# Linear attention in front of an MLP on one core: sub-chunks of 64 tokens in place of 128, with the state advanced twice per chunk

## The chip, the cores and the metric

The kernel runs on one core of a Trainium2 chip. The metric is the device time of one execution in microseconds (us), and the time of a kernel is the median of its runs. The times of this case are of single runs that agree to a few parts in a thousand.

## The reference

Four batches, eight heads, 768 tokens, head dimension 64, all in fp32. Attention is linear and decays by a factor `lam` per head and token. The reference itself goes in blocks of 64 tokens and carries a 64 x 64 state from block to block; its output, with the heads side by side, is the input of an MLP.

```python
for b in range(nb):                      # 12 blocks of 64 tokens
    qb, kb, vb = (q[:, :, sl], k[:, :, sl], v[:, :, sl])
    intra = einsum('bhic,bhjc->bhij', qb, kb) * Dmask[None]      # lam**(i-j) for i >= j, else 0
    intra = einsum('bhij,bhjd->bhid', intra, vb)
    inter = einsum('bhid,bhde->bhie', qb * lam_pow[None], kv_state)
    out[:, :, sl] = intra + inter
    kb_dec = kb * rev_pow[None]
    kv_state = lam_block * kv_state + einsum('bhsd,bhse->bhde', kb_dec, vb)
...
x = out.transpose(0, 2, 1, 3).reshape(3072, 512)
h = x @ w_in                             # 512 -> 2048
out = (h - tanh(h)) @ w_out              # 2048 -> 512
```

## The kernel before

**Stages.** The 768 tokens are cut into six chunks of `BLK` = 128 tokens, and the kernel has six stages g = 0 to 5, one for each chunk of all four batches (512 tokens). In each stage attention makes x for the chunk, and the MLP follows. The MLP's matrix products are done by Strassen and Winograd's scheme of seven products on halves of the operands (`up` for w_in, `down` for w_out), some of them with a second such level inside (`inner_steps` for w_in, `down_twice` for w_out). The sums that the scheme needs are VectorE's (DVE's) work. The products with 128x128 tiles of weights are most of TensorE's (PE's) time. The factors of w_out are kept in DRAM and read again in each stage by GpSimd's (POOL's) queue, `send`, L676 to L696.

**Order.** No planner sets the order. It is the order of the program, written out by hand from L909 to L1086: functions with `yield` (`up_plain`, `down`, `down_twice`, `inner_steps`) are stepped by `next`, `steps` and `every`, and the attention functions stand between the steps. `tied` and `keep_in_program_order` hold an instruction at its place in its engine's queue. In stages from `GB` = 2 on, attention for the next chunk comes in two stretches for two batches each, `att_out(g + 1, (0, 1))` at L1037, after the fourth of `down(g, 2)`'s steps, and `att_out(g + 1, (2, 3))` at L1058, after the seven steps of `down_twice(g, 6)`. In stage 1 the same work for a pair of batches comes in three visits, between `up_plain`'s units (L949 to L972), in stage 0 at the start (L909 to L937).

**One pair of batches.** A matmul of attention is 64 wide in its contraction or its output, and so uses a quarter or a half of the 128x128 array; pairs of heads j = 0, 1 lie on partitions 0 to 63 and 64 to 127. NP = 4 such pairs p. `qt`, `kt` are q and k transposed; in stages 0 and 1 the transposes are PE's (L362) with ACT's copies (L364), later DVE's (L357) from blocked loads. `qd` is `qt` times the powers of lam, `fwd` (L368). The stretch then has, in PE's order:
- scores (`att_scores`, L382 and L384): k's two halves of 64 tokens against q, the first against both halves of q (128 columns), the second against the second alone, into two `sp` banks of tag `att`; DVE multiplies each by `mask` (L388, 128x384) into `ss`;
- state products (`att_read`, L428): `state` against `qd`, 64x64 by 128 columns, into two `op` banks (`ya`, `z`); after them ACT decays the state in place, four ACTIVATEs (L432);
- kv products (`kv_products`, L403): decayed k against v, all 128 tokens deep, into one bank (`yb`); k was decayed by `att_decay` (L394) beforehand;
- inner products (L457, 128 deep, for the second half of the chunk, and L468, 64 deep, for the first), v against `ss`, into the same `op` banks; L468 waits by hand for the first decay (L475);
- DVE adds kv to the state (L477), and ACT copies the `op` banks to `xt` (L479), which the MLP reads; `att_sums` and `inner_tokens` make sums of `xt` for its seven-product schemes.

The last stage has no kv products, no decay of k and loads no k (`nat`, L192).

**PSUM.** There are eight banks: four share the tag `att`, and `ya`, `yb`, `z` and `w` are one each. `down_twice` takes `ya` and `z` or `yb` and `w` for its products n (L780), so that one is read out while the next is made.

**Start.** Weights come as 64-bit words and are rounded in the kernel (`round_block`, L310 to L325, three ACT and some DVE instructions for a block). `mask` is made by eight scans (L110), `fwd` by doubling (`powers`, L116), in stage 1.

Each `nc.tensor.matmul` in fp32 shows in the profile as two MATMUL and two LDWEIGHTS records: 2960 calls make 5856 recorded MATMULs (a few records are missing).

Of the kernel before, what the change touches and what calls it, by code (L numbers as in the profile page):

```python
# [18 lines left out]
BLK = 128  # L19
GB = 2  # L20
# [4 lines left out]
def kernel(  # L25
# [65 lines left out]
    wide = const.tile([128, 192], F32, name="ident")  # L91
    ident = wide[:, 0:128]
    lam_all = const.tile([128, H], F32)
    fwd = const.tile([128, NP, BLK], F32)
    nc.vector.memset(fwd[:, 0, :], 0.0)
# [3 lines left out]

    HALF = BLK // 2
    nc.vector.tensor_copy(wide[:, 128:192], wide[:, 0:64])
    mask = const.tile([128, 2, 6, HALF], F32)
    whole = xpool.tile([128, 3, 2, HB], F32, name="whole", tag="tt").rearrange("s a b c -> s (a b c)")[:, 0:2 * DM].rearrange(
        "s (j p i) -> s j p i", j=2, p=NP)
    for j in range(2):
        for p in range(NP):
            h = 2 * p + j
            nc.vector.tensor_tensor_scan(out=whole[:, j, p, :], data0=lam_all[:, h:h + 1].to_broadcast([128, BLK]),  # L110
                                         data1=ident if p < 2 else wide[:, HALF:HALF + BLK], initial=0.0, op0=AL.mult,
                                         op1=AL.add)
    nc.vector.tensor_copy(mask[:, :, 2:6, :], whole[:, :, :, HALF:BLK])
    nc.vector.tensor_tensor(mask[:, :, 0:2, :], whole[:, :, 0:2, 0:HALF], whole[:, :, 2:4, 0:HALF], op=AL.add)

    def powers():  # L116
        for j in range(2):
            tc.keep_in_program_order(nc.vector.tensor_copy(
                fwd[ts(j, 64), :, 0], lam_all.rearrange("s (p j) -> s j p", j=2)[ts(j, 64), j, :]))
        m = 1  # L120
        while m < BLK:
            tc.keep_in_program_order(nc.vector.tensor_tensor(
                fwd[:, :, m:2 * m], fwd[:, :, 0:m], fwd[:, :, m - 1:m].to_broadcast([128, NP, m]), op=AL.mult))
            m *= 2


    bwd = mask.rearrange("s j p i -> s p j i")[:, 2:6, :, HALF - 1:HALF].to_broadcast([128, NP, 2, D])
# [15 lines left out]
    def load_natural(g, b, names):  # L143
        for name, src, bufs in (("q", q, 2), ("k", k, 3), ("v", v, 4)):
            if name in names:
# [7 lines left out]
                else:  # L153
                    eng = nc.sync if g > 0 else nc.scalar if b == 0 else nc.gpsimd
                    whole_ = {(0, 1, "k"): nc.scalar, (0, 2, "k"): nc.gpsimd}.get((g, b, name), nc.sync)
                    parts = [(eng, x[ts(1 - t, HALF), 4:8], rows[ts(t, HALF), 4:8]) for t in range(2)]
                    parts.insert(2 * (whole_ is nc.gpsimd), (whole_, x[:, 0:4], rows[:, 0:4]))
# [21 lines left out]
    def load(n):  # L179
# [3 lines left out]
        while at["loaded"] < min(n, len(chunks)):  # L183
# [8 lines left out]
            nat = "kv" if g < NG - 1 else "v"  # L192
# [147 lines left out]
    for _ in range(8):  # L340
        nc.tensor.matmul(out=idle[:, 0:128], lhsT=fwd[:, 0, :], rhs=fwd[:, 0, :], start=True, stop=True)


    state = const.tile([128, B, NP, D], F32)


    tr, sc, kdec, xt = {}, {}, {}, {}

    def att_transpose(g, bs):
        for b in bs:  # L350
# [14 lines left out]
            qd = None  # L365
            if g > 0:
                qd = work.tile([128, NP, BLK], F32, name="qd", tag="qd")
                nc.vector.tensor_tensor(qd, qt, fwd, op=AL.mult)  # L368
            tr[g, b] = (qt, kt, qd)

    def att_scores(g, bs):
        for b in bs:
            qt, kt, _ = tr[g, b]

            sp = [bank("sp", "att", 4)[:, 0:6 * HALF].rearrange("s (x i) -> s x i", x=6) for _ in range(2)]
            for p in (0, 2, 1, 3):
                x, r = p % 2, p // 2
                for j in range(2):
                    kj, qj = kt[ts(j, 64), p, :], qt[ts(j, 64), p, :]

                    k0, k1 = (kj[:, ts(t if r == 0 or g >= GB else 1 - t, HALF)] for t in range(2))
                    tied(g != 1, nc.tensor.matmul(out=sp[j][ts(r, HALF), x:3 + p:2 + p - x, :], lhsT=k0,  # L382
                                                  rhs=qj.rearrange("d (t i) -> d t i", t=2), start=True, stop=True))
                    tied(g != 1, nc.tensor.matmul(out=sp[j][ts(1 - r, HALF), 2 + p, :], lhsT=k1,  # L384
                                                  rhs=qj[:, HALF:BLK], start=True, stop=True))
            ss = work.tile([128, 2, 6, HALF], F32, name="ss", tag="ss")
            for j in range(2):
                op = tied(g != 1, nc.vector.tensor_tensor(ss[:, j], sp[j], mask[:, j], op=AL.mult))  # L388
            sc[g, b] = ss
        return op  # L390
# [5 lines left out]
    def kv_products(g, bs):  # L396

        kv = bank("kv", *(("yb", 1) if g >= GB else ("att", 4))).rearrange("d (b p e) -> d b p e", b=2, p=NP)
        for n, b in enumerate(bs):
            kd, vn = raw[g, b]["k"], raw[g, b]["v"]  # L400
            for p in range(NP):
                for j in range(2):
                    tied(g == 0, nc.tensor.matmul(out=kv[ts(j, 64), n, p, :], lhsT=kd[:, 2 * p + j, :],  # L403
                                                  rhs=vn[:, 2 * p + j, :], start=n == 0 and p == 0, stop=True,
                                                  skip_group_check=True))
        return kv

    def att_state(g, bs):
        kv = kv_products(g, bs)
        tied(True, nc.scalar.activation(state[:, bs[0]:bs[0] + 2], kv, AF.Copy))  # L410

    reads = {}

    def out_dst(ops, n, p, j):
        return ops[p // 2][ts(j if p < 2 else 1 - j, 64), p % 2, n, :]

    def att_read(g, bs):
        ops = [bank("op", *x).rearrange("d (p b s) -> d p b s", p=2, b=2)
               for x in ((("ya", 1), ("z", 1)) if g >= GB else (("att", 4),) * 2)]
        decayed = None  # L420
        if g > 0:
            st = state[:, bs[0]:bs[0] + 2]
            for n, b in enumerate(bs):
                for p in (0, 1):
                    for j in range(2):
                        r = ts(j, 64)
                        for pp in (p, p + 2):
                            nc.tensor.matmul(out=out_dst(ops, n, pp, j), lhsT=state[r, b, pp, :],  # L428
                                             rhs=tr[g, b][2][r, pp, :], start=n == 0 and p == 0, stop=False,
                                             skip_group_check=True)  # L430
            for p in (3, 2, 1, 0):
                op = tied(g == 1, nc.scalar.activation(st[:, :, p, :], st[:, :, p, :], AF.Copy,  # L432
                                                       scale=fwd[:, p, BLK - 1:BLK]))
                decayed = decayed or op
        reads[g, bs] = ops, decayed

    def att_out(g, bs):
        half = bs[0] // 2
        xt[g, half] = xpool.tile([128, KI, HB], F32, name=f"xt{half}", tag=f"xt{half}")
        st = state[:, bs[0]:bs[0] + 2]  # L440
        if g >= GB:

            att_scores(g, bs)
        if (g, bs) not in reads:
            att_read(g, bs)
        ops, decayed = reads.pop((g, bs))

        def dst(n, p, j):
            return out_dst(ops, n, p, j)

        if g >= GB:
            kv = kv_products(g, bs) if g < NG - 1 else None
        for n, b in enumerate(bs):
            ss, vn = sc[g, b], raw[g, b]["v"]
            for p in range(NP):
                for j in range(2):
# [660 lines left out]
```

## Time and profile before

| | |
|---|---|
| median of 3 runs | 659.21 us (657.57 to 659.94) |
| the profiled execution | 658.74 us, of which its span in the trace is 657.0 |
| PE, matmuls | 644.1 us busy, 98% of the span |
| PE, weight loads (beside the matmuls) | 590.7 us, 90% |
| DVE | 468.9 us, 71% |
| ACT | 243.7 us, 37% |
| POOL | 209.0 us, 32% |
| granted TensorE clock | 0.995 mean |
| instruction transfers (queue q8) | 47, 0.77 MB |

How PE's busy time lies over the stages, in us of each stretch of the span:

| from to | length | PE busy |
|---|---|---|
| 0 to 30 (start, stage 0) | 30.0 | 24.5 |
| 30 to 115 | 85.0 | 84.4 |
| 115 to 213 | 98.0 | 97.9 |
| 213 to 328 | 115.0 | 112.7 |
| 328 to 434 | 106.0 | 105.3 |
| 434 to 540 | 106.0 | 106.0 |
| 540 to 657 | 117.0 | 113.4 |

Times in lines of the trace count from the span's start. A line of PE's timeline gives start, length, engine, source line, operation, tiles as output<-moving,weights, the shape of the part of the array and of the data, and a count; what stands in brackets is the idle time before it and what ended it. The length of one matmul contains the time in which it lies in the pipe (L468's mean is 226 ns, though one starts every 15 to 20 ns), so the cost of a group of matmuls is read from start to start. "issue" as a releaser means that the engine waited for nothing that the profile shows.

### The profile page before, as it was taken

What the parts mean: (1) busy time and instruction counts of PE and PEld (TensorE: products, weight loads), DVE (VectorE), ACT (ScalarE), POOL (GpSimd) and SP (SyncE); (2) the same over time, 40 slices, a digit from 0 to 9 for tenths busy, and PEclk for the clock granted to TensorE, in tenths of its full rate; (3) what the DMA queues carried; (4) which work ended last, traced back from release to release, by engine and by line L of the source; (5) the groups of instructions that cost most, each with busy time, mean ns of one, the idle gap of its engine ahead of it and who ended that gap; (6) DMA issues with size and microseconds to landing.
All of it is one profiled execution on the core that took longest, in us unless ns stands there. A gap on an engine that the chain in (4) does not pass through costs nothing. (4 is left out here: it accounts for less than half of the span.)

```text
span 657.0 us, 15041 instructions
## 1 busy us (share of the span) xinstructions
PE 644.1 (98%) x5856; PEld 590.7 (90%) x5856; DVE 468.9 (71%) x889; ACT 243.7 (37%) x485; POOL 209.0 (32%) x362
## 2 busy tenths in 40 slices
PE   8899999999999999999999999999999999999998
PEld 7788888888888899988999988999988899998897
DVE  4457979968878785578776668789468687466663
ACT  2776766523321222532223452213453213263210
POOL 6000126766223335202335302243401164400241
PEclk7999999999999999999999999999999999999999
DMA  9869987988768768957656957576967476721374
GB/s 201 198 168 200 254 245 229 380 245 253 146 143 212 212 182 257 211 95 187 198 173 213 243 125 168 141 242 200 238 123 159 113 268 209 225 71 33 89 247 162
DMA packets 156951, 125.80 MB, mean 191 GB/s; under 512 B 127744, under 2 KB 130048, under 8 KB 156880
## 3 DMA queue, kind: packets, MB, share of 16 engines
q0 software_dynamic: 27168, 87.91, 43.8%
q1 hardware_dynamic: 128096, 36.53, 26.8%
q8 instruction: 47, 0.77, 0.5%
q10 hardware_dynamic: 1616, 0.39, 0.4%
q14 instruction: 24, 0.20, 0.1%
HBM read 103.81 MB, written 20.97 MB: 190 GB/s over the span
## 5 line engine op out<-in xcount | busy, mean ns | idle before, releaser
L691 POOL DMA_DIRECT2D wb<-fine x148 | 79.7, 539 | 189.8 <-PE y L788 63.2
L792 ACT ACTIVATE q<-y 128x128 f32<-128x128 f32 x96 | 26.6, 277 | 144.4 <-PE y L788 143.4
L788 PE MATMUL y<-wb,g 128*128 128x128 f32 x456 | 60.3, 277 | 0.7 <-DVE q L802 0.7
L843 PE MATMUL h<-xt,w 128*128 128x256 f32 x256 | 58.0, 383 | 2.0 <-DVE w L325 2.0
L843 PEld LDWEIGHTS h<-xt,w 128*128 128x128 f32 x256 | 47.6, 190 | 9.9 <-DVE w L325 3.2
L788 PEld LDWEIGHTS y<-wb,g 128*128 128x128 f32 x456 | 55.3, 192 | 1.2 <-issue 0.6
L694 POOL DMA_DIRECT2D wb<-factors x44 | 23.8, 541 | 83.1 <-PE y L733 50.8
L556 ACT ACTIVATE th<-g 128x512 f32<-128x512 f32 x40 | 25.2, 630 | 66.6 <-DVE g L574 50.7
L548 PE MATMUL y<-xt,w 128*128 128x256 f32 x192 | 45.0, 379 | 0.0
L388 DVE TENSOR_TENSOR ss<-sp,mask 128x384 f32<-128x384 f32 x48 | 23.7, 550 | 26.4 <-PE sp L384 26.4
L557 DVE TENSOR_TENSOR g<-g,th 128x512 f32<-128x512 f32 x40 | 27.6, 691 | 20.7 <-ACT th L556 20.7
L548 PEld LDWEIGHTS y<-xt,w 128*128 128x128 f32 x192 | 36.4, 190 | 5.1 <-ACT g L565 0.2
L788 PE MATMUL zw<-wb,g 128*128 128x128 f32 x304 | 40.3, 275 | 0.0
L548 PE MATMUL y<-tt,ws 128*128 128x256 f32 x160 | 37.8, 379 | 0.0
L548 PE MATMUL y<-tt,w 128*128 128x256 f32 x160 | 37.8, 379 | 0.0
L548 PE MATMUL z<-xt,ws 128*128 128x256 f32 x160 | 37.8, 379 | 0.0
L733 PE MATMUL y<-wb,g 128*128 128x256 f32 x160 | 37.3, 379 | 0.0
L788 PEld LDWEIGHTS zw<-wb,g 128*128 128x128 f32 x304 | 37.0, 192 | 0.2 <-DVE g L794 0.2
L733 PE MATMUL w<-wb,g 128*128 128x256 f32 x160 | 35.3, 379 | 0.0
L548 PEld LDWEIGHTS z<-xt,ws 128*128 128x128 f32 x160 | 30.4, 190 | 4.1
L733 PEld LDWEIGHTS y<-wb,g 128*128 128x128 f32 x160 | 30.4, 190 | 4.1
L733 PEld LDWEIGHTS w<-wb,g 128*128 128x128 f32 x160 | 30.4, 190 | 4.1
(206 smaller groups left out, 1469.4 us busy)
## 6 DMA issues: line engine op xcount, KB each, us to landing
wb<-fine POOLq DMA_DIRECT2D x148, 256.0 KB, 3.9
wb<-factors POOLq DMA_DIRECT2D x44, 256.0 KB, 4.7
wb<-fine_in POOLq DMA_DIRECT2D x36, 256.0 KB, 4.0
raw<-in_moe_w_out_dram SPq DMA_DIRECT2D x12, 512.0 KB, 6.4
rest<-fine POOLq DMA_DIRECT2D x20, 256.0 KB, 4.6
raw<-in_moe_w_in_dram SPq DMA_DIRECT2D x16, 256.0 KB, 6.4
fine<-f POOLq DMA_DIRECT2D x16, 256.0 KB, 4.7
q_blk<-in_q_dram SPq DMA_DIRECT2D x128, 32.0 KB, 3.3
```

The costliest lines, as they stand in the source:

```text
L388: op = tied(g != 1, nc.vector.tensor_tensor(ss[:, j], sp[j], mask[:, j], op=AL.mult))
L548: nc.tensor.matmul(out=t[:, m, :], lhsT=wt[:, kt, ts(m, 128)], rhs=x[:, kt, :], start=first and m == 0 and kt == 0, stop=kt == 1, skip_gro ...
L556: nc.scalar.activation(th, src, AF.Tanh)
L557: nc.vector.tensor_tensor(dst(c), src, th, op=AL.subtract)
L691: nc.gpsimd.dma_start(out=t.rearrange("p m c -> p (m c)"), in_=fine[TWICE.index(n_), SUB.index(x_)].rearrange("p u c -> p (u c)"))
L694: nc.gpsimd.dma_start(out=t, in_=factors[XAT[FACT[n_][1]]][:, 2 * x_:2 * x_ + 2, :])
L733: nc.tensor.matmul(out=t[:, m, :], lhsT=a[:, u, kt, ts(m, 128)], rhs=wb[:, kt, :], start=first and u == 0 and m == 0 and kt == 0, stop=u = ...
L788: tied(x == STEPS[-1], nc.tensor.matmul(out=dst, lhsT=a[:, u, :], rhs=wb[:, ts(u, 128)], start=x in (1, 2) and u == 0, stop=u == NU - 1, s ...
L792: nc.scalar.activation(keep, dst, AF.Copy)
L843: tied(u == 0, nc.tensor.matmul(out=hm[c][:, m, :], lhsT=w1[u][:, i, a, ts(m, 128)], rhs=xt[0, t][:, i, :], start=m == 0 and i == 0, stop= ...
```

## The change

Attention goes in sub-chunks of `HALF` = 64 tokens, like the reference; the stages stay at 128.
- `mask` and `fwd` are made for 64 tokens; scores are only those within a half, 16 products of 64x64x64 for each batch, and `ss` is 256 wide in place of 384. `row(j, t)` puts half t of head j on one half of the partitions, and k and v are loaded with the halves of the odd heads swapped. `fwd` is made at the start.
- `kv_products` makes the kv of each half of the chunk, in two banks, all as quarter products.
- `att_half` does the first half of a chunk: state products, four decays by ACT, scores (from stage 2 on), kv, inner products, and DVE's addition of the first kv to the state (a copy by ACT in stage 0). `att_out` then does inner and state products of the second half with the new state, and ACT's copies to `xt`. `att_state` comes later: four more decays, and the second kv is added.
- From stage 2 on the two halves of the output have two banks each: `ya` and `z` for the first, two `att` banks for the second. `down_twice`'s products 4 and 7 use `att` banks, so that kv can have `yb` and `w`.
- The last stage does kv for its first half, and so loads and decays k.
- `att_state` and part of `inner_tokens` are placed between the MLP's steps; the decay of k for the pairs of stage 1 and the first pair of stage 2 moves ahead.

```diff
-    fwd = const.tile([128, NP, BLK], F32)
+    fwd = const.tile([128, NP, HALF], F32)
+    state = const.tile([128, B, NP, D], F32)
...
-            nat = "kv" if g < NG - 1 else "v"
+            nat = "kv"
...
+    def row(j, t):
+        return ts(j if t else 1 - j, HALF)
...
-            for p in (0, 2, 1, 3):
-                x, r = p % 2, p // 2
-                for j in range(2):
-                    kj, qj = kt[ts(j, 64), p, :], qt[ts(j, 64), p, :]
-                    k0, k1 = (kj[:, ts(t if r == 0 or g >= GB else 1 - t, HALF)] for t in range(2))
-                    tied(g != 1, nc.tensor.matmul(out=sp[j][ts(r, HALF), x:3 + p:2 + p - x, :], lhsT=k0,
-                                                  rhs=qj.rearrange("d (t i) -> d t i", t=2), start=True, stop=True))
-                    tied(g != 1, nc.tensor.matmul(out=sp[j][ts(1 - r, HALF), 2 + p, :], lhsT=k1,
-                                                  rhs=qj[:, HALF:BLK], start=True, stop=True))
+            for p in range(NP):
+                for t in range(2):
+                    for j in range(2):
+                        kj, qj = kt[ts(j, 64), p, :], qt[ts(j, 64), p, :]
+                        tied(g != 1, nc.tensor.matmul(
+                            out=sp[j][row(j, t), p, :], lhsT=kj[:, ts(t, HALF) if g >= GB else row(j, t)],
+                            rhs=qj[:, ts(t, HALF)], start=True, stop=True))
...
+        tags = (("z", 1), ("w", 1)) if (g, bs) == (0, (0, 1)) else (("yb", 1), ("w", 1)) if g >= GB else (("att", 4),) * 2
+        kv = [bank("kv", *x).rearrange("d (b p e) -> d b p e", b=2, p=NP) for x in tags[:2 if g < NG - 1 else 1]]
...
+                for t in range(len(kv)):
+                    for j in range(2):
+                        tied(g != 1, nc.tensor.matmul(
+                            out=kv[t][ts(j, 64), n, p, :], lhsT=kd[row(j, t), 2 * p + j, :],
+                            rhs=vn[row(j, t), 2 * p + j, :], start=n == 0 and p == 0, stop=True, skip_group_check=True))
...
+    def out_banks(g, t=0):
+        def both(tags):
+            return [bank("op", *x) for x in tags]
+        if g >= GB:
+            two = both((("att", 4),) * 2 if t else (("ya", 1), ("z", 1)))
+            return None, [[x[:, 0:4 * HALF].rearrange("d (p b s) -> d p b s", p=2, b=2) for x in two]]
+        pair_ = both((("att", 4),) * 2)
+        views = [x.rearrange("d (p b s) -> d p b s", p=2, b=2) for x in pair_]
+        return views, [[x[:, :, :, ts(t, HALF)] for x in views] for t in range(2)]
+    def in_quarters(g, bs, make):
+        for n, b in enumerate(bs):
+            for p in (0, 1):
                 for j in range(2):
+                    for pp in (p, p + 2):
+                        op = tied(g != 1, make(n, b, pp, j, n == 0 and p == 0))
+        return op
+    def state_products(g, bs, ops, t):
+        return in_quarters(g, bs, lambda n, b, p, j, first: nc.tensor.matmul(
+            out=out_dst(ops, t, n, p, j), lhsT=state[ts(j, 64), b, p, :], rhs=tr[g, b][2][ts(j, 64), p, ts(t, HALF)],
+            start=t == 0 and first, stop=False, skip_group_check=True))
+    def inner_products(g, bs, ops, t, after=None):
...
+                out=out_dst(ops, t, n, p, j), lhsT=raw[g, b]["v"][row(j, t), 2 * p + j, :], rhs=sc[g, b][row(j, t), j, p, :],
...
+    def att_half(g, bs):
+        st = state[:, bs[0]:bs[0] + 2]
+        banks_, ops = out_banks(g)
         decayed = None
         if g > 0:
+            state_products(g, bs, ops, 0)
+            decayed = decay_state(g, bs)
+        if g >= GB:
+            att_scores(g, bs)
+        kv = kv_products(g, bs)
+        op = inner_products(g, bs, ops, 0, decayed)
+        if g == 0:
+            made = tied(True, nc.scalar.activation(st, kv[0], AF.Copy))
+        else:
+            made = tied(g >= GB, nc.vector.tensor_tensor(st, st, kv[0], op=AL.add))
...
     def att_out(g, bs):
...
+        if g >= GB:
+            att_half(g, bs)
         xt[g, half] = xpool.tile([128, KI, HB], F32, name=f"xt{half}", tag=f"xt{half}")
+        banks_, ops, kv = half_way[g, bs]
+        if g >= GB:
+            ops += out_banks(g, 1)[1]
+            inner_products(g, bs, ops, 1)
+            state_products(g, bs, ops, 1)
+        else:
+            state_products(g, bs, ops, 1)
+            inner_products(g, bs, ops, 1)
...
+    def att_state(g, bs):
+        if g == NG - 1:
+            return
...
+            decay_state(g, bs)
+        tied(g != 1, nc.vector.tensor_tensor(st, st, half_way[g, bs][2][1], op=AL.add))
...
     def down_twice(g, n):
...
-        y, zw = (("ya", "z") if n in (4, 6) else ("yb", "w")) if g == NG - 1 else ("ya", "z") if n in (5, 3) else ("yb", "w")
-        y, zw = bank("y2", y, 1)[:, 0:128], bank("zw", zw, 1)
+        if g == NG - 1:
+            y, zw = ("ya", "z") if n in (4, 6) else ("yb", "w")
+        else:
+            y, zw = {4: ("att", "att"), 7: ("att", "att"), 6: ("yb", "w")}.get(n, ("ya", "z"))
+        y, zw = bank("y2", y, 4 if y == "att" else 1)[:, 0:128], bank("zw", zw, 4 if zw == "att" else 1)
...
+        if not last and g < GI:
+            att_decays(g + 1, (0, 1))
         p2 = down(g, 2)
         steps(p2, NU)
         send(stream.index((g, 4, SUB[0])))
-        if not last and g < GI:
-            att_decays(g + 1, (0, 1))
+        next(p2)
         if not last:
             att_out(g + 1, (0, 1))
         every(p2)
         sums_twice(g, 5)
         p4 = down_twice(g, 4)
+        steps(p4, 3)
+        if not last:
+            att_state(g + 1, (0, 1))
...
+        if not last:
+            inner_tokens(g + 1, False)
         p6, p7 = down_twice(g, 6), down_twice(g, 7)
-        steps(p6, len(STEPS))
+        steps(p6, len(STEPS) + 1)
         if not last:
             att_out(g + 1, (2, 3))
         every(p6)
         steps(p7, 2)
         if not last:
+            att_state(g + 1, (2, 3))
             att_sums(g + 1, None)
```

## The prediction

> **What bounds the kernel now.** I read the page first, parts 1 and 2, for the engine that sets the end.
>
> ```profile
> span 657.0 us, 15041 instructions
> ...
> PE 644.1 (98%) x5856; PEld 590.7 (90%) x5856; DVE 468.9 (71%) x889; ACT 243.7 (37%) x485; POOL 209.0 (32%) x362
> ...
> PEclk7999999999999999999999999999999999999999
> ...
> q8 instruction: 47, 0.77, 0.5%
> ```
>
> TensorE (PE) is busy 98% of the span at full clock, so a change pays what it takes from PE or leaves PE waiting. The last line is used below: 47 transfers of 16 KB carry instructions, and 2 x 5856 records of PE over 47 is 249 per transfer, so they are in the main PE's own.
>
> The chain of waits runs along PE through every attention stretch (L382, L428, L403, L457, L468 one after the other). So I took PE's timeline for one such stretch, stage 4, second pair of batches; columns are start, length, engine, line, tiles, shapes, count.
>
> ```profile
> 441.95 0.32 PE L382 MATMUL sp<-qt,kt 64*64 64x128 f32 x1
> ...
> 443.33 1.05 PE L428 MATMUL op<-qd,state 64*64 64x128 f32 x32
> 444.32 1.15 PE L403 MATMUL kv<-v_nat,k_nat 128*64 128x64 f32 x32
> 445.30 1.10 PE L457 MATMUL op<-ss,v_nat 128*64 128x64 f32 x32
> 446.34 0.69 PE L468 MATMUL op<-ss,v_nat 64*64 64x64 f32 x32
> 446.96 0.60 PE L788 MATMUL y<-wb,g 128*128 128x128 f32 x3
> ```
>
> From start to start: scores 1.38 us, state 0.99, kv 0.98, tall inner products 1.04, short ones 0.62; 5.01 us for 192 records. Then the same view one stage earlier and in the last stage, where a stretch is longer:
>
> ```profile
> 342.99 0.34 PE L468 MATMUL op<-ss,v_nat 64*64 64x64 f32 x7
> 343.99 0.62 PE L468 MATMUL op<-ss,v_nat 64*64 64x64 f32 x25 [0.66 <-issue]
> ```
>
> ```profile
> 547.05 0.56 PE L468 MATMUL op<-ss,v_nat 64*64 64x64 f32 x21
> 548.00 0.45 PE L468 MATMUL op<-ss,v_nat 64*64 64x64 f32 x11 [0.38 <-issue]
> ```
>
> In the middle of one line's matmuls PE stood 0.66 and 0.38 us, released by "issue": no semaphore, no data. The transfer view around these moments has one instruction transfer each, 341.14 to 342.66 and 545.81 to 546.75. PE went on 1.33 and 1.25 us after their ends. A third pause of 0.74 us (241.29) also ends 1.26 us after such a transfer (239.07 to 240.03), though the profile names a DVE op there. I read these as PE having run out of instructions.
>
> **Part A, PE's work.** After the change all four products are 64x64x64 on quarters of the array. A pair of batches has 64 matmuls of each kind in two records: 4 x 64 = 256 records. Price: inside L468 the records' starts come in fours 6 to 8 ns apart, with a new four every 58 to 59 ns (446.70, 446.76, 446.81), so 14.6 ns a record. Entering the form costs some 0.05 us and leaving it 0.09 (L468's last start to L788's first is 0.148). So 256 x 14.6 = 3.73, + 0.14 = 3.87 us. The other bound is L468's whole group, 0.62/32 = 19.4 ns, 4.97 us; I take 14.6, since the kinds now follow each other in one form.
> - Stages 2 to 4, six stretches: 5.01 - 3.87 = 1.14 each, **-6.8**.
> - Last stage, two: now 4.23 (520.10 to 524.33, no kv). After: 192 x 14.6 = 2.80, and 32 kv records that use two quarters only, 58 ns per two as in L403, 0.93; with 0.14 3.87. **-0.7**.
> - Stage 1, two pairs, each in three visits: now 1.50 + 1.03 + 2.64 = 5.17; after 3.73 + 3 x 0.14 = 4.15. **-2.0**.
>
> Sum **-9.5**.
>
> **Part B, instructions.** A matmul call is two records and two weight loads, four instructions; 2960 calls now, 3344 after. A transfer holds some 256 instructions, 128 records. At the products of the MLP these last 128 x 0.112 = 14 us (L788: eight records in 0.89). In a stretch now they last 128 x 5.01/192 = 3.3 us; after, 128 x 14.6 ns = **1.87**. How fast can they come? After each of the three pauses, PE has just begun a block and the next transfer begins 1.59, 1.47 and 1.31 us later (345.58, 549.47, 242.60), takes 1.19, 1.33 and 1.20, and by the pauses the instructions can run 1.25 to 1.33 after its end: 4.1, 4.1 and 3.8 us from block to block. So a block that lies wholly in a stretch should cost 4.0 - 3.3 = 0.7 now (0.66, 0.38, 0.74 seen) and 4.0 - 1.87 = **2.1** after. A stretch now is 384 instructions, one and a half blocks, so some stretches hold no whole block; a stretch after is 512, two blocks, so each holds at least one. The block that sticks out brings its own cover, since beyond the stretch 64 instructions take 3.5 us. Stepping blocks of 256 through the program's order with these paces gives 14 to 24 us over the eight stretches by where the boundaries fall, about 17 in the middle. What is lost now goes out of this: 0.66 + 0.38 + 0.74, and 0.26 by which L468 at 213.48 (0.95) is longer than its usual 0.69: 2.0. **+15**, between +12 and +22. Stage 1 has at most 320 fast instructions in a row, and slow products around them: 0 to 1, taken as 0.
>
> **Part C, waits that the order adds.** The second half's state products wait for a DVE add (new L471) of the state, behind four ACT decays.
> - Stages 2 to 5: the decays (1.26 to 1.28 for four, L432) run beside scores; the mask products, four of 0.33 now that they are 256 wide (L801 has that size), end about when kv does; the add needs 0.6; PE meanwhile has 0.93 of inner products. 0 to 0.2 a stretch; behind the add are only DVE's MLP sums, due later. In the first stretch of stage 2, kv's second bank waits for the sum L759, and DVE is busy to 210.1: 0.3.
> - Stage 1, first pair: ACT now rounds to 74.0, decays 1.26, rounds again; DVE's first op on the w_out block stands ahead of the add in its queue, which so ends near 78.0. PE, with 3.46 us of products between, asks at 77.5: 0.5. Second pair: ACT reaches the decays at 95.09, behind the rounding L320 to L322; PE asks at 94.8: 0.6. DVE is held to 97.6 by L325 and L862, the add ends at 98.3, PE asks at 97.65: 0.7.
>
> Sum 2.2; a stretch that waits for instructions hides a part. **+1.5**, between 0 and 4.
>
> **Part D, at nothing.** Start: PE waits there for others (1.26 at 21.70 and 0.40 at 27.76, both for rounded weights behind ACT). The new state copy and products on ACT's way to the first xt (0.6 + 0.5) stand against 0.7 saved on products; one more block of instructions comes into these 20 us (64 calls). **+0.5**, from -1 to +2. DVE: 48 mask products shorter by 0.14; ten adds of 0.6, four decays in the last stage, four qd halves and two state products more: +4 in 188 us idle. ACT: eight more sets of decays and split copies, +13 in 413 idle. SP issues 12 more k loads in the last stage; k of 64 to 128 KB lands in 3.7 to 3.9, and its first reader is two units of products later. Products 4 and 7 go to the att banks, which DVE's mask products have freed by then; if not, up to the 0.74 seen at 241.29 each. POOL's weight loads follow PE's reads and shift with them. The token sums that move ahead, and the stage-1 decays, lie in DVE's idle time; if that cover goes, the wait at 227.3 (1.54, DVE L794) grows by 0.7.
>
> **Sum** on the profiled execution (658.74, span 657.0; 0.5 under the median 659.21): 658.74 - 9.5 + 15 + 1.5 + 0.5 = 666.2, near the median **666.5**.
>
> **Rivals.**
> 1. Instructions keep up (other side). Mechanism: the pauses come from something else, or a deeper store of instructions is filled between stretches, 14 us per block being ample. It decides from the point where more than two blocks are held. Then 658.74 - 9.5 + 1.5 + 0.5: **651**. Against: 47 transfers x 249 cover all of PE's records, so hardly any reserve is loaded at the start. The skill (Runtime: NRT & Kernel Launch, Instruction fetch mechanics) says that fetching is mostly hidden behind issue, and gives PE room for 2048 instructions, eight blocks; the two "issue" pauses speak against it.
> 2. The loss is halved: the transfers are later now because the stretches coincide with weight transfers (DMA 0.7 busy at 338 to 344.6) and come 0.9 us sooner after. 7 to 8 less: **659**, no change.
> 3. Quarter products run at 19.4 ns. Two row halves write one bank in the new inner products. Nothing gained on the six, +0.7 each on the last two, blocks 2.5 us, so 1.5 x 8 - 2.0 for them, and 2.0 from C and D: **672**. Against: L428 does the same now, 32 records of double width in 0.99. The skill (TensorEngine Tiling (Array Packing), Gotcha 1) forbids just this at one time; L428's 31 ns for four-fold packing shows no price.
> 4. DVE is late for the adds in every stretch, 1 us: **673**.
>
> **How the numbers follow.** Own case 0.60 (660 to 674 by its bounds), rival 1 0.20, rival 2 0.10, rival 3 0.06, rival 4 0.04. About 0.5%, 3.3 us, is what a measurement can tell from no change. Slower than 662.5: 0.52 of mine and 0.10 of rivals 3 and 4. Same: 0.08 of mine and 0.10. Faster: 0.20. The range for 8 in 10 goes from 650 (into rival 1) to 674.
>
> **What would show it.** PE's timeline of a stretch: fours every 58 ns, and pauses "issue" of about 2 us, one in nearly every stretch, ended 1.3 us after an instruction transfer; some 53 such transfers. A stretch of 3.9 us without a pause proves rival 1; fours at 78 ns rival 3; pauses ended by L471 rival 4. Wrong most likely if the transfers' 4.0 us, seen three times, is not the rule.

## The result and the profile after

The changed kernel takes **675.38 us** (median of 4 runs, 673.03 to 678.0) against 658.39 of the kernel before beside it; the ratio is 1.0261, 95% interval 1.0212 to 1.0311. It is slower, as forecast, but by 17.0 us where 7.3 were forecast, and 1.4 us above the range. The profiled execution is 675.85 us, its span 674.0.

The page of the changed kernel, the lines that answer to those shown of before:

```profile
span 674.0 us, 16685 instructions
...
PE 645.5 (96%) x6624; PEld 592.4 (88%) x6624; DVE 472.5 (70%) x908; ACT 254.7 (38%) x533; POOL 209.5 (31%) x362
...
PEclk7899999999999999999999999999999998999999
...
q8 instruction: 53, 0.87, 0.6%
```

PE's busy time has not fallen, though its products are smaller; its share has, and the clock row has one slice of 8 (the mean clock is 0.985, 0.995 before). What PE waited for, from its waits (us in total, times, longest):

```profile
PE op L431 <- issue: 9.3, 4, 3.8
PE op L437 <- issue: 2.9, 2, 1.9
PE h L882 <- DVE w L321: 2.3, 2, 1.9
PE y L826 <- issue: 1.7, 2, 1.0
PE kv L402 <- issue: 1.7, 3, 1.1
PE kv L402 <- DVE ss L382: 1.6, 1, 1.6
```

"issue" heads the list, and the added state sum (L471) is not in it. The kernel before has 1.6 us of "issue" in all:

```profile
PE op L468 <- issue: 1.0, 2, 0.7
...
PE sp L382 <- issue: 0.6, 1, 0.6
```

One stretch of the changed kernel, stage 3's second pair, in PE's timeline:

```profile
343.87 0.69 PE L431 MATMUL op<-qd,state 64*64 64x64 f32 x32
344.38 1.11 PE L377 MATMUL sp<-qt,kt 64*64 64x64 f32 x64
345.33 1.49 PE L402 MATMUL kv<-v_nat,k_nat 64*64 64x64 f32 x62
...
347.64 0.34 PE L431 MATMUL op<-qd,state 64*64 64x64 f32 x6
351.80 0.67 PE L431 MATMUL op<-qd,state 64*64 64x64 f32 x26 [3.82 <-issue]
352.41 1.43 PE L826 MATMUL y<-wb,g 128*128 128x128 f32 x8
353.63 1.91 PE L826 MATMUL zw<-wb,g 128*128 128x128 f32 x8
355.34 1.64 PE L826 MATMUL y<-wb,s 128*128 128x128 f32 x8
```

Two things are to be seen. PE stops for 3.82 us after six of 32 records of one line. And behind the pause the MLP's eight records, 1.06 long elsewhere, are 1.43, 1.91 and 1.64 long. The windows view of the same place gives the reason (window, its length, PE, PEld, DVE, ACT and POOL busy with counts, granted clock, DMA share, GB/s):

```profile
343.80:347.90 4.10, 4.10 (x232) 3.93 (x230) 2.63 (x7) 2.06 (x7) 1.27 (x3) 1.00 0.92 293
347.90:351.70 3.80, 0.08 (x6) 0.00 (x0) 1.58 (x3) 0.15 (x1) 0.00 (x0) 1.00 0.15 57
...
353.30:355.30 2.00, 2.00 (x11) 2.00 (x11) 0.00 (x0) 1.12 (x4) 0.54 (x1) 0.50 0.04 8
...
457.80:460.00 2.20, 0.34 (x19) 0.20 (x12) 2.17 (x4) 0.66 (x2) 0.00 (x0) 1.00 0.01 6
460.00:463.00 3.00, 3.00 (x72) 2.93 (x72) 0.06 (x2) 1.98 (x7) 0.54 (x1) 1.00 0.02 5
```

After the pause the clock is 0.50: 11 records in 2.0 us, where full speed does 18. In the trace it is at half for 3.41 us, from 353.15 to 356.56, and again after the pauses of 2.14 us (to 433.50) and 1.60 us (to 563.75). After the pause of 1.86 us that ends at 459.93 it is not: those are the last two lines.

**Where the time went.** I took the start of the MLP's first w_in product in each stage from both traces, and in between the sums of PE's start-to-start times. After less before:

| | us |
|---|---|
| up to stage 1's MLP (stages 0 and 1 of attention) | +3.7 |
| from there to stage 5's, the eight stretches: | +13.7 |
| - between attention's own records, without pauses | -3.4 |
| - entries into and exits from the stretches | -0.5 |
| - pauses inside a stretch (1.78 before, with the 0.74 at the exit at 241.29; 11.80 after) | +10.0 |
| - pauses elsewhere (1.54 before; 3.45 after, of which 1.71 "issue" just behind a stretch) | +1.9 |
| - between the records of the inner scheme of w_out, 4.8 of it right behind three pauses (half clock) | +5.6 |
| PE's products from there to their end (stage 5) | 0.0 |
| from PE's last product to the end | -0.3 |

### The profile page after: what moved, and what is told of

The parts are those of the page before. It is cut to its first block, busy times and chain, and to the rows that moved or that the text cites. A ratio compares the mean times of both kernels' runs of the same rounds, so it can differ in the third digit from the quotient of the medians.

```text
span 674.0 us, 16685 instructions
## 1 busy us (share of the span) xinstructions
PE 645.5 (96%) x6624; PEld 592.4 (88%) x6624; DVE 472.5 (70%) x908; ACT 254.7 (38%) x533; POOL 209.5 (31%) x362
## 4 chain that ended last, share of the span: by engine, by line
PE 87%; issue 5%; DVE 4%; ACT 2%; DMA 1%; POOL 0%; DVEq 0%; POOLq 0%; ACTq 0%
PE y L575 16%; PE y L826 12%; PE zw L826 9%; PE y L666 6%; PE h L882 6%; PE z L575 6%; PE w L767 5%; PE y L767 5%; PE acc L912 4%; PE z L666 3%; PE kv L402 2%; PE op L431 2%; PE op L437 2%; PE sp L377 2%; PE w L666 2%
## 5 line engine op out<-in xcount | busy, mean ns | idle before, releaser
L826 PE MATMUL zw<-wb,g 128*128 128x128 f32 x304 | 42.8, 286 | 1.0 <-DVE g L832 0.7
L826 PEld LDWEIGHTS zw<-wb,g 128*128 128x128 f32 x304 | 39.2, 201 | 1.5 <-DVE g L832 0.9
L449 ACT ACTIVATE state<-state,fwd 128x128 f32<-128x128 f32 x72 | 24.2, 395 | 34.6 <-PE op L431 34.6
```

The costliest lines, as they stand in the source:

```text
L449: ops = [tied(g == 1, nc.scalar.activation(st[:, :, p, :], st[:, :, p, :], AF.Copy, scale=fwd[:, p, HALF - 1:HALF])) for p in (3, 2, 1, 0)]
L826: tied(x == STEPS[-1], nc.tensor.matmul(out=dst, lhsT=a[:, u, :], rhs=wb[:, ts(u, 128)], start=x in (1, 2) and u == 0, stop=u == NU - 1, s ...
```

## The experiments

**Theory:** PE runs out of instructions at the ends of blocks of 256, and a pause so made costs a second time, since the clock falls for 3.41 us. **Rivals:** the pauses are waits of the new order that the trace does not name; the clock falls by what attention does, not by idle time.

**e4_more: only more instructions.** The kernel before, its order and banks untouched, with the products of 128 columns made as two of 64 (L428 likewise).

```diff
-    tied(g != 1, nc.tensor.matmul(out=sp[j][ts(r, HALF), x:3 + p:2 + p - x, :], lhsT=k0,
-                                  rhs=qj.rearrange("d (t i) -> d t i", t=2), start=True, stop=True))
+    for t, y in enumerate((x, 2 + p)):
+        tied(g != 1, nc.tensor.matmul(out=sp[j][ts(r, HALF), y, :], lhsT=k0, rhs=qj[:, ts(t, HALF)],
+                                      start=True, stop=True))
```

> The kernel before, with its order, waits and banks as they were, but the products of 128 columns (scores L382, state products L428) each made as two of 64 columns: 192 records of a stretch become 256, as after the change, at the same array time. Theory (instructions): pauses 'issue' in nearly every stretch, 8 to 13 us in all, and a drop or two of the clock: 665 to 672. Rival (order, waits and banks of the change cost the time): 658 to 660, as before.

Measured: 669.09 us, ratio 1.0151 (1.0122 to 1.0181). PE's timeline of stage 3's second pair:

```profile
342.67 0.45 PE L404 MATMUL kv<-v_nat,k_nat 128*64 128x64 f32 x8
345.28 1.17 PE L404 MATMUL kv<-v_nat,k_nat 128*64 128x64 f32 x24 [2.16 <-issue]
346.13 2.02 PE L459 MATMUL op<-ss,v_nat 128*64 128x64 f32 x32
348.08 1.13 PE L470 MATMUL op<-ss,v_nat 64*64 64x64 f32 x32
```

There is a pause in the middle of kv, which here waits for nothing new, and there is half clock behind it (L459 2.02 long, 1.10 in the kernel before). Seven such pauses make 9.1 us (one of them, 1.14 us, goes by the name of a DVE op, though it ends 1.42 us after an instruction transfer like the rest); from stage 1 to stage 5 the kernel loses 12.9 us. More instructions alone do nearly what the whole change does there, so the rival that named waits of the new order falls.

**e1_shift: the blocks moved.** The changed kernel with 32 small matmuls at its start.

```diff
+    for n in range(32):
+        r = ts(n % 2, 64)
+        nc.tensor.matmul(out=idle[r, 128:192], lhsT=none[r, 0:64], rhs=none[r, 64:128], start=True, stop=True)
```

> The changed kernel with 32 small matmuls more at its very start, 128 instructions of TensorE that write nothing that is read; all that follows is as it was. Theory (TensorE runs out of instructions at the ends of blocks of 256): every pause 'issue' of the eight stretches moves by 64 matmul records, since the ends of the blocks do: in the stretches 2 to 8 it leaves kv (L402), the second state products (L431) or the first product behind the stretch, and stands in or next to the inner products (now L440) or kv, and each still ends 1.2 to 1.5 us after an instruction transfer; pauses of 10 to 17 us in all, time 668 to 680. Rival (a wait of the new order, on data or a bank, that the trace does not name): the pauses stay with the lines where they were, second state products and kv.

Measured: 672.26 us (1.0205, 1.0168 to 1.0243). The same stretch as above:

```profile
348.90 1.36 PE L405 MATMUL kv<-v_nat,k_nat 64*64 64x64 f32 x62
...
350.11 0.33 PE L440 MATMUL op<-ss,v_nat 64*64 64x64 f32 x4
352.03 1.09 PE L440 MATMUL op<-ss,v_nat 64*64 64x64 f32 x57 [1.60 <-issue]
...
353.57 1.16 PE L829 MATMUL y<-wb,g 128*128 128x128 f32 x8
```

The pause now stands 64 records earlier, at the start of the inner products, as it should; in six of the eight stretches it is in L440. So nothing in those lines made PE wait. The instructions of PE's queue can be counted in the traces (matmul records, weight loads and semaphore waits; no record is missing, since each of the 64 transposes makes one matmul record, and 2 x 2960 - 64 is 5856). By this count the nine "issue" pauses in and behind the stretches of the changed kernel, the nine of e1_shift, the seven of e4_more and the three of the kernel before all end 191 or 192 instructions past a multiple of 256. e1_shift is also a control for the clock. In its profile the clock did not fall in these stages (mean 0.997). From stage 1 to 5 it loses 5.5 us, 8.2 less than the changed kernel: 5.4 of this lies between the records of the inner scheme, where the half clock was, and most of the rest in shorter pauses. The profiled execution is the fastest of four (669.24 to 675.81).

**e7_run: the disputed cost by itself.** The kernel before with runs of 64, 128, 256 and 32 quarter products in the MLP, one run in each of the stages 2 to 5.

```diff
+    def quick(n):
+        a, b = bank("quick", "att", 4), bank("quick", "att", 4)
+        for i in range(n):
+            r, c = i % 2, (i // 2) % 2
+            tc.keep_in_program_order(nc.tensor.matmul(
+                out=(a, b)[r][ts(c, 64), 0:64], lhsT=state[ts(r, 64), 0, c, :], rhs=state[ts(r, 64), 1, c, :],
+                start=True, stop=True, skip_group_check=True))
```

> The kernel before with runs of quarter products (64x64x64, on data that is there, written to banks that nobody reads) behind the up products of the stages 2 to 5: 64, 128, 256 and 32 calls, which are 256, 512, 1024 and 128 instructions, far from attention and without any wait. At 58 ns for four records they take 1.9, 3.7, 7.5 and 0.9 us, 14.0 in all. Theory (blocks of 256 instructions can't come faster than one in about 4.0 us): the run of 1024 takes 13 to 17 us and has three or four pauses about one block (128 records) apart, each ended 1.2 to 1.5 us after an instruction transfer; that of 512 takes 5 to 8, those of 256 and 128 at most 2 more than their due; 684 in all. Rival (instructions keep up, the pauses are attention's own waits): 7.5 us for the 1024, and 672.

Measured: 678.46 us, in one run. The run of 256 calls:

```profile
521.61 4.12 PE L823 MATMUL quick<-state 64*64 64x64 f32 x265
526.54 2.09 PE L823 MATMUL quick<-state 64*64 64x64 f32 x128 [0.82 <-issue]
530.00 1.98 PE L823 MATMUL quick<-state 64*64 64x64 f32 x119 [1.36 <-issue]
```

Two pauses, 128 records apart: one block of 256 instructions. The runs take 2.0, 5.6, 10.3 and 1.1 us, where 1.9, 3.7, 7.5 and 0.9 are due: the pauses are there, but smaller than expected (10.3, not 13 to 17). From 526.54 to 530.00 a block takes 3.46 us, with the DMA engines 0.02 busy, not 4.0. In the stretches of the changed kernel, where weights come in, seven of the nine blocks that end in a pause take 3.3 to 4.4 us, one 2.5 and one 6.2: in this last the instruction transfer began 3.7 us after the block, as against 0.8 to 2.2 at the seven, behind 4 us of DMA at 0.92. That the weights held it up is likely by this; it wasn't tried by itself.

**e2_pauses and e5_pauses: pauses without a lack of instructions.** The kernel before, with ACT copies between two steps of the inner scheme (1, 2, 3, 4, 2, 3, 4, 5, 3 and 6 of them).

```diff
+            if x == 7 and (g, n) in PAUSES:
...
+                for i in range(PAUSES[g, n]):
+                    held = tc.keep_in_program_order(nc.scalar.activation(...a11, AF.Copy))
+                    if i == 0:
+                        wait_for(held, op)
...
+                if held is not None:
+                    wait_for(op, held)
```

> The kernel before, with ten pauses of TensorE made on purpose in the MLP, far from attention: ahead of one step of the inner seven-product scheme of w_out (products 4 and 5 of every stage) the matmuls wait for 1 to 6 ACT copies of 128x512 (0.63 us each), which wait for the matmul before. Theory (a pause of some 2 us that falls into one window of 3.4 us halves the granted clock for the next 3.4 us): the pauses of 1 or 2 copies (0.7 to 1.5 us) leave the clock at 1.00, those of 4 to 6 copies (2.6 to 4 us) are each followed by a stretch of 3.4 us at 0.50, those of 3 copies (2.0 us) by chance of the window; span 657 + 24 of pauses + 1.7 for each drop, 5 to 8 of them: 690 to 695. Rival (the clock falls only with what goes on in an attention stretch, such as small products): no drop, and 681.

A miss: 661.24 us in one run, because PE did not pause. The later steps' products, not bound to their place, were put ahead of the waiting ones, and covered all but 0.3 us. It tells nothing of the clock. With all of that scheme's products bound to their order:

> The kernel before with ten pauses of TensorE made on purpose, as in the run with pauses before this one, but with all products of the inner scheme of w_out held in their order, so that no later product fills the pause: the matmuls of one step wait for 1 to 6 ACT copies of 0.63 us, 33 copies in all. Theory (a window of 3.4 us in which TensorE is busy less than about half is followed by one of 3.4 us at half clock): the pauses of 1 and 2 copies (0.8 and 1.5 us with the way there and back) leave the clock at 1.00; those of 4, 5 and 6 (2.7 to 4 us), four in number, are all followed by 3.4 us at 0.50 unless the pause falls half into each of two windows; those of 3 copies (2.1 us) in some of three cases. Span 657 + 24 + 1.7 for each of 3 to 7 drops: 686 to 693. Rival (the clock fell only through attention's small products): no drop, 681.

Measured: 693.63 us in one run, span 691.9. PE waited 22.5 us for the copies in ten pauses. Four of them, each with the stretch behind it, from the windows view:

```profile
328.70:330.80 2.10, 0.06 (x2) 0.04 (x1) 1.93 (x3) 1.89 (x3) 0.54 (x1) 1.00 1.07 300
331.60:335.00 3.40, 3.40 (x19) 3.40 (x19) 0.78 (x2) 0.28 (x1) 1.07 (x2) 0.54 0.31 89
...
439.30:440.70 1.40, 0.03 (x1) 0.00 (x0) 1.23 (x2) 1.26 (x2) 0.54 (x1) 1.00 0.98 305
440.80:445.00 4.20, 4.20 (x38) 4.20 (x39) 2.76 (x7) 0.83 (x3) 1.61 (x3) 1.00 0.74 236
...
447.20:449.30 2.10, 0.06 (x2) 0.03 (x1) 2.10 (x5) 1.89 (x3) 0.00 (x0) 1.00 0.02 10
449.40:454.00 4.60, 4.60 (x42) 4.60 (x43) 4.53 (x12) 0.83 (x3) 2.15 (x4) 1.00 0.32 114
...
553.80:557.30 3.50, 0.13 (x2) 0.09 (x1) 3.50 (x8) 3.15 (x5) 0.88 (x2) 0.90 0.85 277
557.30:563.60 6.30, 6.30 (x30) 6.30 (x31) 2.44 (x8) 0.55 (x2) 1.61 (x3) 0.51 0.30 93
```

A pause of 2.04 us halves the clock at 328.7 and does not at 447.2; one of 1.38 does not; one of 3.37 does for two spells. All spells of half clock that lie whole in the twelve traces are 3.41 us or twice that, and begin on one grid of 3.41 us in each trace. I reckoned PE's busy share in each cell of that grid that ran at full clock, past the start. Shares of 0.40 and less were always followed by half clock, shares from 0.54 never; between them it went both ways. From stage 1's MLP on the kernel is 31.5 us longer than before. The waiting is 22.5, and the records of the scheme in which the pauses lie take 12.5 more between them, most of it in seven cells at half clock; against this most of the 3.3 us of pauses that the kernel before had there went away. Attention has no part in these pauses, so the rival on the clock falls.

**e3_spread, e6_onecut, e9_halves, e10_spread2: the stretch cut up**, so that slow products lie between the small ones. All products stay. e3 cuts each stretch in three:

```diff
-        steps(p6, len(STEPS) + 1)
-        if not last:
-            att_out(g + 1, (2, 3))
-        every(p6)
-        steps(p7, 2)
+        steps(p6, len(STEPS) - 1)
+        if not last:
+            att_begin(g + 1, (2, 3))
+        steps(p6, 2)
+        next(p7)
+        if not last:
+            att_half(g + 1, (2, 3))
+        steps(p7, 2)
+        if not last:
+            att_out(g + 1, (2, 3))
+        every(p6)
+        steps(p7, 1)
```

`att_begin` is the state products, decays and scores of `att_half`; the first pair is cut alike, around `p2` and `p4`.

> The changed kernel, all of its products as they are, but each of the eight stretches of the stages 2 to 5 cut in three (first state products and scores; kv and first inner products; the second half) with one or two steps of the MLP's products between them. Theory (TensorE runs out of instructions, then the clock falls): blocks now last 3.3 us and more, pauses shrink from 13.6 us to under 4, the clock does not fall in these stages; against that two more entries and exits of 0.14 us per stretch, 2.2 in all: 675.4 - 10 - 1.8 - 4.8 + 2.2, about 661, from 654 to 665. Rival (the waits that the new order brings, for the mask products and the state's addition): pauses named after DVE come in place, and the time stays over 670.

Measured: 668.56 us (1.0146, 1.0119 to 1.0172), 6.8 below the changed kernel but not the 661 expected. The pauses went as they should: inside the stretches 0.12 us is left of 11.80 (and 0.6 behind one), and the clock stays up past the first stage. In their place PE waits for DVE:

```profile
PE zw L833 <- DVE gS L839: 3.2, 4, 1.1
PE op L431 <- issue: 2.1, 2, 1.5
PE h L889 <- DVE w L321: 1.8, 2, 1.5
```

Without pauses attention's own records take 31.1 us from stage 1 to stage 5, against 38.2 before: this is what the smaller products are worth, **7.0 us**. It is spent. Entries into and exits from the pieces take 8.9, which is 5.2 more than in the kernel before and 5.6 more than in the changed kernel. Less the 0.11 that lies between two of the MLP's records anyhow, each of the 16 further visits costs 0.24 us, 3.9 in all, where 2.2 were expected. The rest and more goes to waits of the MLP's products that stand close behind (4.9 against 1.5 before, most of it for DVE), and to 2.4 us of gaps under 0.15 us between the records of the inner scheme, whose cause is open.

e6 takes one of the two cuts back.

> The run with stretches cut in three, with one of the two cuts taken back: the first state products and scores stand ahead of the last step of the MLP product before, all the rest (160 records, 320 instructions) behind it in one piece. Theory: a piece of 320 instructions in 2.4 us can still hold a whole block, so pauses 'issue' of 0.3 to 1.6 us come back in about five of the eight stretches, 4 to 7 us in all, with at most one drop of the clock; one exit and entry less saves 0.25 x 8 = 2.0, and DVE's lateness behind products 4 and 7 (some 3 us with both cuts) mostly goes: 668 to 671, about where three pieces stand and below the 675.4 of the change. Rival (what is left over the kernel before comes from cutting alone): 663 to 665.

Measured: 675.44 us (1.0272, 1.0212 to 1.0331), worse than expected. "issue" is back with 12.0 us over the whole kernel, 5.4 of it in the stages 0 and 1, which were not touched (2.69 and 2.75 where the changed kernel has 1.76 and 0.33 at the same lines). These two end 1.36 and 1.20 us after an instruction transfer, so how much a stage loses depends on when a transfer lands. Besides, kv, now at the head of its piece, waits 3.9 us for DVE and ACT (L800, L837, L847).

e9 cuts in the middle; e10 is e3 with DVE's work in another order; both also move two pieces of the stages 0 and 1 apart:

```diff
-    steps(unit, 1)
+    steps(unit, 2)
     att_out(0, (2, 3))
...
-... (att_scores, 1, (2,))]),
-             (3, (22,), 1, [(att_scores, 1, (3,))])]
+... (att_scores, 1, (2, 3))]),
+             (3, (22,), 1, ())]
```

> The changed kernel with each stretch cut once, in the middle: first state products, scores and the first batch's kv (128 records), then two steps of the MLP's products (1.8 us), then the rest (128 records). Besides, in the stages 0 and 1 two pieces of attention are put further apart (a second step of up products ahead of stage 0's last piece; the last scores of stage 1 one unit earlier). Theory: neither piece holds a whole block of 256 instructions unless the ends fall together, but a block that reaches over the cut has only 1.8 us of slow products, and lasts some 3.4 us, about as long as the next block takes to come: pauses 'issue' of 2 to 6 us in all, no drop of the clock; one exit and entry more is 0.25 x 8 = 2.0: 675.4 - 11 - 4.8 + 2 - 2 = 659.6, from 657 to 665. Rival (cutting alone costs what it saves, as the run with one cut behind the scores): 668 to 675.

> The run with stretches cut in three, with DVE's work around it put in an order that is not late (the transposes for the next chunk behind the sums for the product in hand, the sums for product 5 ahead of the second half), and with the two edits in the stages 0 and 1 of the run beside it. Theory: no pause 'issue' is left in the stages 2 to 5, and DVE's lateness (some 5 us behind products 4 and 5 in the run with three pieces) mostly goes, and 1.6 of the wait for the mask products of stage 1: 668.6 - 4 - 1.6 - 1 = 662, from 658 to 665: about 7 us of smaller products gained, some 5.6 of it given back for two exits and entries more in each stretch. Rival (what remained was not DVE's lateness): 666 to 669.

Measured: 675.03 (1.026, 1.0223 to 1.0298) and 671.52 (1.0219, 1.0179 to 1.0259): both misses. The edit in stage 0 made PE wait for rounded weights (4.1 and 4.2 us in all, 1.8 in e3), and DVE's lateness did not go, it moved:

```profile
PE zw L833 <- DVE g L839: 5.4, 3, 2.4
PE h L889 <- DVE w L321: 4.2, 3, 2.2
PE kv L402 <- issue: 1.9, 1, 1.9
PE sp L377 <- ACT kt L357: 1.9, 3, 0.7
PE op L431 <- issue: 1.7, 2, 1.3
PE zw L833 <- DVE tt L653: 1.6, 1, 1.6
```

These are e10's lines. The first is another operand of the same line as in e3, and its pause of 2.38 us drew half clock for 6.83 us, from 241.92 on. In e9 a wait of 3.30 us for the same operand did the same, from 240.67 on.

**e8_before_shift:** the kernel before with e1's 32 matmuls.

> The kernel before with 32 small matmuls more at its very start (128 instructions that write nothing that is read), which move the ends of TensorE's blocks by half a block against attention. Theory (blocks): the pauses 'issue' of 0.66, 0.38 and 0.74 us that the kernel before had in or behind its stretches go; at most one of 0.3 us comes in their place; 656 to 658.5, 0.5 to 2 us below the kernel before, hardly more than the measurement can tell. Rival (pauses belong to the lines where they stood): they stay, in L468's inner products (now L471), and the time is unchanged or 1 us longer for the added matmuls.

Measured: 658.11 us, ratio 0.9997 (0.9969 to 1.0024). The three pauses went, and one "issue" of 0.2 us is left in the stretches. In the profiled execution, the slowest of twelve, a wait for DVE of 1.54 us before is 2.46 us here, with half clock behind it; whether this takes up the gain in the others is not shown. The time is the same within the interval. No version here beats the kernel before.

## Why the prediction was wrong

**The sign and the bound were right.** PE ran out of instructions, and this decided. **Part A** was right for the stretches: -7.5 forecast for all eight (-6.8 and -0.7), and -7.5 measured. The measured sum is put together from two runs: -7.0 of attention's own records, as e3 has them without pauses, and -0.5 of entries and exits in the changed kernel. The fours come every 58 ns (kv at 428.868, .926, .985). The one stretch without a pause inside (534.03 to 538.08) takes 4.05 us where 3.87 stood. **Part B** was right in size, if not in its constant: +15 net forecast for the stretches; measured are 10.0 of pauses inside, 1.7 behind, and 3.6 that lie hidden in attention's own sums, by difference (-3.4 there against the -7.0 of e3): 15.3. Of the 3.6, 1.5 is the draining of the last records before seven pauses, 0.22 us each, before the profile counts idle time; the other 2.1 lies spread over the records and is not shown to be a lack of instructions. That the sum came so near is in part luck. The single pauses are 0.23 to 3.82 us where 2.1 stood for each, and with the blocks moved (e1_shift) the same account gives 12.0. Most blocks come every 3.3 to 4.4 us, not 4.0 throughout; with the DMA engines free, 3.46.

**What failed is the price of a pause.** Part B charged a pause with its own length, 4.0 - 1.87, and the sum had no term for what idle time does to the clock; the forecast said only that the clock was full. Three spells of half clock cost some 1.6 us each behind the stretches, 4.8 in all. A fourth, at 22.05 to 25.47, fell into stage 0, behind 1.92 us of waiting for rounded weights; it cost up to 1.7. The kernel before shows half clock only at its start (8.8 to 15.6 us); the first digit of its clock row, 7, could have been asked what brought it about, and was not. The Trainium skill (TensorE: Matmul & The Clock Gate, Part 1) has the mechanism: a free-running window of about 3.4 us sets the clock to half or full. The runs agree with its window, 3.41 us. Its rule that about one idle window brings the clock down is looser than what is measured here: 1.60 us in one cell were enough.

**The second miss is stages 0 and 1:** "0 to 1, taken as 0" in Part B and +0.5 in Part D. The trace has pauses "issue" of 1.76 us (state products of stage 0's second pair, 29.07) and 0.33 us (kv, 75.4), with their drains 2.5 (the kernel before has one of 0.57 in stage 0, at 18.85). Part A's -2.0 and C's 1.3 for the second pair hold roughly: PE waited 1.57 us, though for the mask products that had to leave kv's banks (L382), not for the added sum.

Put together: 666.2 + 4.8 + 1.7 (clock) + 2.5 = 675.2, and the profiled execution is 675.85. This is a sum of parts, and the 1.7 is an upper bound. The table of the result says the same from start to start: +13.7 in the stretches, where Parts A and B come to +7.5, and +3.7 in the stages 0 and 1, where Parts A, C and D come to about 0.

**The rivals.** "Instructions keep up" is dead by e7_run and e4_more. The Trainium skill (Runtime: NRT & Kernel Launch, Instruction fetch mechanics), which would have given this rival its ground, says fetching is mostly hidden; here it is not, with 53 transfers for the 13,538 instructions of PE's queue that the trace holds. Ten blocks of 256 in the stretches held under 3 us of work (2.0 to 2.9), and nine of them ended in a pause. "The loss is halved" (659) went the other way: in the stretch where weight transfers held DMA at 0.92, the loss was the largest, 3.82 us. Quarter products at 19.4 ns and a DVE that is late for each sum are not there: no wait for L471 is listed.

**The range** failed by the missing term: its upper end, 674, was Part B's end with nothing behind it.

## What to carry to other kernels

Count instructions as well as array time: where products get smaller, work out how long 256 instructions last, and compare with the time between the transfers that bring them (3.3 to 4.4 us here). Then price idle time of PE twice. Three pauses here left PE busy for 0.39, 0.46 and 0.53 of a cell of 3.41 us, and each cost some 1.6 us more behind it; other cells with shares between 0.44 and 0.53 cost nothing more, so this can be bounded, not foretold. Cutting each dense piece in three with slow products between did away with both in the stretches (a single cut did not), but each cut has its own entry and exit (0.24 us net here), and moves the queues of the other engines.

## What the runs showed of the hardware

- PE's instructions come in blocks of 256, one transfer each. In the stretches of the changed kernel the next transfer began 1.1 to 2.0 us after PE had gone on from a pause into a new block. The transfers that PE waited for took 0.9 to 1.6 us, and PE went on 1.2 to 1.5 us after their end.
- Half clock comes in spells of 3.41 us on a grid that does not start with the kernel, so executions of one program can lose different amounts. The four of the changed kernel took 673.03 us (mean clock 0.995), 674.9 (0.985), 675.85 (0.985) and 678.0 (0.990): the clock alone does not put them in order.
- Quarter products of 64x64x64 run at 14.6 ns a record on the four quarters, also where two halves of the rows write one bank (kv in the changed kernel, 428.87 to 429.16).
